# The ending of a fused attention and gated-MLP kernel: one bank for the last P V sum, two row tiles held in PSUM, stores from ScalarE, and a new written order

## The chip, the cores and the metric

The kernel runs on one core of a Trainium2 chip. The metric is the device time of one execution in microseconds. Before the change it was 691.36 us (median of 3 runs, 690.31 to 693.7).

## What is computed

With `x` of 2048 x 512 in bf16, 32 heads of 16 and a hidden width of 1792, the reference normalises each row and adds an attention block and a gated MLP block to the input:

```python
xn = layernorm(x)
q, k, v = split(xn @ wqkv)                      # 32 heads of 16
p = softmax(q @ k.T * 16 ** -0.5)               # per head, 2048 x 2048
attn = (p @ v) @ wo
h = relu(xn @ W_gate) * (xn @ W_up)
out = x + attn + h @ W_down
```

## The kernel before

Queries are taken in four chunks of 512 (`c4`), heads in four groups (`gg`) and in each the even and odd heads (`ee`): 32 blocks. In each block the keys go in 16 tiles of 128 (`kt`). TensorE works in "ops" of four matmuls of 64 rows by 32 columns, with one half of its rows (`half` 0 or 1, written by `matmul_loaded`, line 250); the two halves run side by side. Most key tiles are done as two *units*: two score ops write two PSUM banks (tiles `s`, two such pairs of banks), ScalarE takes the exponential of both banks in one instruction (line 1375) into a ring in SBUF, and two P V ops of each pair of units add to the block's sum. Other key tiles are *quads*: the exponential is made from integer arithmetic, by VectorE out of PSUM (line 1330), and then twice with a shift, on VectorE (line 1349) or GpSimd (line 1345); three times two P V ops use the results. There are 718 units.

The rest of TensorE's work, projections of q, k and v, gate and up (`gu`, `gg`) and the output rows (`ob`), is put between the scores. It shares four PSUM banks (pool `P_b`) with the quads' scores and the P V sums. Output row tiles of 128 queries sum the 14 parts of `h @ W_down` and four of `attn @ wo`, and the residual is added when VectorE takes them out.

The order of every engine's instructions is written out: `PLAN` is a packed list in which the operations that the code records are placed, with the buffer number of each tile. `Graph.run` reads it; `Graph.emit` adds the semaphores, and lets TensorE wait when an op of one half adds to a bank that the other half wrote last.

The ending (`normalise_last`, lines 1122 to 1181) belongs to the last block and the four row tiles of the last chunk:

- `LAST2 = 1`: the last block's P V sum is kept in two banks, one for each half (`tp`, `tp_hi`). ScalarE copies the one to SBUF (line 1148), VectorE adds the other (line 1150), each in two pieces of 256 queries.
- VectorE transposes in blocks of 32 (line 1153), takes reciprocals of the sums (1154), spreads them by a second transpose (1155) and multiplies (1157) into `qf`.
- All four row tiles were begun earlier (`out_rows`, `RN - 1` steps ahead of the end): the MLP parts and two head groups, taken out to `resid(i)` in fp32 together with `x` (line 1061). At the end two further groups (`oT`) and the normalised last one (`qf`) are projected by `stream_out` (line 1183) into the score banks `finA`, `finB`.
- Row 3 (`TAIL_ACT = (3,)`) gets its residual by an fp32 matmul with an identity matrix (line 1133) and is taken out by ScalarE (line 1171); rows 0 to 2 are added to their residual on VectorE (line 1174).
- SP issues the four stores (line 1179). Ahead of the last `LAST_STORES` entries of its queue it waits for all its other streams (line 498).

Of the kernel before, what the change touches and what calls it, by code (L numbers as in the profile page):

```python
# [13 lines left out]
ACTF = mybir.ActivationFunctionType  # L14
ALU = mybir.AluOpType

S = 2048
D = 512
H = 32
# [19 lines left out]
LAST_STORES = 4  # L39
# [15 lines left out]
LAST2 = 1  # L55
TAIL_ACT = (3,)
# [65 lines left out]
PLAN_OPS = 8251  # L122
PLAN = (
    "c-n1S1z;3c*PZibve|?P-r(+~K+zK1H53RgAq1zmLkq#JcySHx1oxuBixj8DwYa1-B)jwe``*m#&hq_5vOD|azANXP`<5z-?|)qU;npkhm-SBk%JG0+=1?9OFU$$t_)PpZ9&?`sx#E46{UQBP9-7;D"
    "=UY><D-W!Pig#D;eI!lD@z7?SVte7W#hl8mH{2Y<&EH({?qk_vJk!1JbU6Uxh2039E8-c%vSJ}9=1|2uRL+(k$TwoF?)3*vle5jk`|RXB47Z)yv>w(`bYn$sZK+tBadS6gynJfzO!nxW@#3W%C*Hxc"
    "ndc<Zc%8%A0<@vrlU5V2<p?fc$c16c1<%op4Qx@OC)|n$yk0f-l-r20y6IiHJv_N#`igVzO&o6d%sho*yJ47cl5RRc7|&g*VX%1=V+#)H9wQ*S&tK-YhNrk`mN3eg%&l{apQbZ~&E|n%_{j_vJ#(qL"
    "xrwyPo^@8V%qUxd;I?08&KMgT>sqNt&yBn^?6TZui>Y@5g?kFlc<;5*zK+~aJaj{*h+NNY#aa5(*g{w-=P8~-)6MvEFLIb$nihDA&-_ehT<qkr+8n1d`BZvZymYBzTW0KFd~TjdSf(&ru5s^CVXJcK"
    "RGMu*)0JdZ1cMn-;o>KqQhX#{x|w018>X>t=7zLNF6cIg%lU3$wtPS@nOn@43%E@ix#>g8|Gq~0;-IVnCOjz?7Uwm6&5ivm=ef<Gh!@f-Zfs{5F1%xyXyl3<z|GUjI3+9G&+s;6Qo?k%*ukwBM=-ZF"
    "wi0vQ=0@^k={C=~L}0%7*+JcljEap>JQ;75zaktfgX(6+AF;lhK4hk!6%%y0X9Rc40+Zzk6Aa8vbZ{Fncru?nDJMfNV5}iZg_&S1kL1ByGrEj}jAK^(4QowbTHE=Q1tc6v_lw%0K}im(e9#}$@j9d#"
    "w1``7W~7?P8pEZA>#Z0XhFd3>Kind}xM`)^f<422Yg5yFSjKwT!&aBx^y3~bv%#p1c;rX?KYu03UtvZ{ySZhK=@wz7=_=EcrhB+mMr7-kK$lp~JgB*pfvW%c3kq->Mwr$cCb%V6FuNKc&$!`13DZwr"  # L130
    "KoG_ln8CU7Rl+FD#z<}>V#W}zo7F9oO$Lb@Oy$98-AsF$!u2Gl;)N|w&Jd+=CSh1SW88vP4-c3&$gK^!qXW8CxjO8mDbb31M3{{%%}4O&tBXl1-Cvwv!@ZXVIJb!;?qvrb81igp{cRT^Uiwh%WNcg9"
    "qiuZFv#T|0F!!nti9lYY(CyMkx5-gUs+iDXI@wnIx)<>cZ_2eilq?s6$AhMLfK3b9>*Oo_YVHir@ja)~&EfFTY*xs=QhMe((7jY(LYqAvcI|Cty>3GtYfso5<Pk`UO|bfmvxJ0V-_S$JG6trYG$sll"
    "h2qgzoPVX6y+Jlt5WevHg0E8MD_XX3pGWg@?jxOTTE)_L7EgOnfm>{4(U3)wZtJH&U`xUnU}%)N#a+f8;<3(rgsLDqD~Q&{ZkU8?aFb*<YnBub@F6nYKofW{*VbHdPmvib7-?<DIsvN|hH?{7JhW?!"
    ";T~|em`6g1xt1Y2EtE6i%&a(WE@zzIKrZo?d|;f=l)Y|6F(sg+53YM%PV~jC_?m=fY;8<eEHPy;odt6S|H2rpc#zImSFv%wCI1bE<`z&|OUkj_FxsX2nI`KNLYs>lde#zj+)__wBA8Khd)gOce?!D6"
    "-WE&rN|txIQL@aCTZ$Juy@+byyyER3xYXfB=U_=LuBC9@t$9nq&29aOxA%}81$=5vHy{#Lhhvc|M4Bm3d^%LF*!y0Oru3Z0RQ$G+dnK`z^PU#hI+7VYGjw*KG=-1iZEk$jgGV5Fouhciac?mzwnR~M"
    "PwNU3`xR>qt6{NH5*FGk%2z<j?TxKzgSUg?RySqzGsY-xCM>t|*2f)YV+^k$rmnXT$j$(|oyiUM&_(DtcWE{U+3z|$ROZ9Ewo`E*8uvoF4Z!S|A<9={xDO0@KC!LttpM9eyo_Q2nn}1Y!9mAY*G9TW"
    "4#1OG#v)#KaZevBk>2b(J)B@#=W(h>F(f&doh41LNFL?pe&)*Hw)-d}XJn*3J9vf~lT49kp2#ki$=)P?FWm{L$$dK-#ix1o`PfFB);N1ZY>8~^uE{3Uz4^d>T6sGG+t;wfm0fb#<(iKbc7U-r$=vpo"
    "dm3@WCEUv?rg|40fL&I5FkOcY11zHER<k5A$3sz8S1a3i8?hRCiyPQ%u4qVgPy6fL$O1E1_-3)3hb0ZT<=)1@rXTSCl#}_^twXfo+@Yj+F~s^|Zsny<t0yoa-o$5%tY8N+DMj3t_HtXdZ1&SyTHiu%"
    "&yARQzr;=da_^;<mkxF7R?X;%JtPee(D}Mh_w*MQ{c+E&pA8H=O^=Zl9<^Za2W*PR7fS3&Y5=@(Il_IK4=azDM>AMGr`(;Jj*}6$dUaDc**Mo0An7=h>ukwkiyE_u4AUMvf!J=%cnV_{ohhdFGsKjU"
    ";)+Lf=$`cBp61V_eCw*vWLCMXMs}O`dL{{Zu3W9ev4U!a&$@r`5H`F-CC=xeFxwTQbq#8<w#8nyYe-8;dNhZX1G)*Ba)NGguSaAlU*FgJP?opN@=~rv!2c^CylCVBGhYc|-iTUv)0PypF`bV^+{T6}"  # L140
    "+SkNpmk!+9)Y$LrxSdXXNRs<>jMg@~?+rM&ci6V0amDvr79T@=klafQP`<L;D>FP_S$KOrPh)IAxWTDV{vUerwBPcT=dQtGeb`*4+nC<Q`d&gc?>!8($5&U<y0_uB)xEv;b!%tiX8J2y;^wyq_A5S*"
    "W$?sK_jZxo?t0yP2TNOWZo4n`Dlg+k)&3op&n3xM{LU4xLv{GveOTwyVRJUO-Q#@q6_ocH#rGCnw{A7K_5F>MBC^!2t1)g~eVG^8Ci$5cjn>Vs+um0i;A!=Q%yxmOSeI~&TNktj_>zi}&6Vf&O|fpA"
    "ty^kOZo94Coxx??HhVJKxYe}o#Ke`aX^5pbOqjPIUAI~m?g0zqytc0#yeaMZuFSZbfCtR%z-N73<i&6acHDDSZr$+dibaZ^mPhy82iaOT4+~ffWVR@V%2iCbGnmR~;e41{u{U=f3Q)kkU}q4x`Td^M"
    "xhB*Yt10;ZC8=*K!0j++YnZ@&uETu3KJ~O9%2)Vff9cbC_~ItFe+O#2jDz=EWZ&<8?f7P|GmfvAL9t!SnU`wb!&-1?C5LgdWsDPE{NF}Q@zE+i;A0e@r=o4&+xawDHstobjQyW6#+{12v-=9$^%OrJ"
    "p5WXLdR{cNU-)vLcz?~s_AA@3zht+k3IFQy+2#c$9en?L<bWgPU#O&&SrMqZs_JKpYg)h;RS!tU+fdD4eS&m&lL7u>ct*|b@2205>$$bR7@p>$XMQgFi_uRpAjJKarDyDBZq322;sJer4|##?456PG"
    "QqeXlzf|&ES)8RkaTWDhrIkR=N+&C^y|fDbq+dt^s<Q=USg5W|@4%Kv0VN!FfLsp8M@_uQ=FmR;1BChAep!D{Eth=cOmtpJNvw9H=4&8Rvijzmmk7mK*WQSBt4Hzse`&pb0ZyXcUK|?_Xbi(Av%#}~"
    "Pu=SvatqqVH^!$#_|NMb1ibY-z}fYAz<FFKjZ?2P`~-~prVRF^)!(IM<w^s?TCr7HyYGSiZC!y&R6Y7NtB7MYfOAQj^RtsioJe*$-9G?5TRK+g-IL1#2SS#+Sa(<K1z^`NwGK7-{zo8Q`=#EFT7g?1"
    "0%w~t2O0DyP(auEcPZ3=3L75@Ov%dbWq)#Z2e55k^r{xoK%EwA+Npk8b71AN4l6q?@IM3$DZp+Qxl&Y3-3eIrLfex7jMp-}OAH(ejM(#|7W7v4!$@F0-fn9&3MkeTY<=66H-NG0XY}%4azGmaOiU?t"
    "Ds`f^0_c?a$uNxD0J7%59~~FuoCY-0x+bj}j1uBisf*nML5D9h<=A$Xa~tq|&O3SU<;P~AXqkvn_-$2tQ~;ubSf5cLiLoeoF)u>UCeiUZBvCyJRPfi5aRjKg@?H>9em)FTnufHUk|+JF{tj$+rlCao"
    "_9jV1^5aC;P2EvoI`A6F9a0Le0$My;i(&V&UjjlM)gR@+ok0Eb6<`ngkN?F{lm;a99)l5+-6t#YAp<)AMSf$w=Tt^9@^Q!H!<Uo7_cG}9o&xPt{HI{Zm$mfji^}MXC`#$t!R5d##y|dY1}GmF?OHs4"  # L150
    "A<%sRdY>ugf2KklW!m?3Ci#`vN`}lvCp|!04@5v+-*!shoxo%CoSF)UY5_U!xqF-h9<=Pbd}E~g$3x`6Xss>cW&*p1Yn$Jp{lZ%L{>E`MZg`|J)xZxgvOjV8WqR#m>#HBB7RFr}_N1k!XK-r3Enu=X"
    "SNGRCP&f;^60onzF%)fe6UciK6<r;dINQ$!?mi0?Rg8MT@4fe;){<`5LCeQ1bF5~c5-K0Anm`k>1mntMRDT3y){kTC&d1r|JceJ!G5*V8l6(9m*0KT6rcjQ2(ry*Li*Kn43O+z4?PGD^C^9|S-~CPI"
    "O80=QY<MGFZ#UxXDzR36*WZO*4;Xp%Att_0Q*(W*gRdWFxliLBE?UR5<&+NRkop5I-)g;aLfF%+c)7HlwsZz?@fBvYa<j~sF@ZL?{3!EV>}cntH2YJZ?PMKU`m4zL3@w4?U5X<m3-Aw;t~zcOP=m{j"
    "8HF)jF!v|qe&j|jgtcAUQr{c^+(EV{$iQw^rNP&eg7T{wfgOPhyQRF_(0574MV)E`Eql)Dm(+|3kxuzJ^+!i5+V8dlB`&L+|2v1O=PA-ZKUw7JYP}0>Jx<fxBDt{`{#k3jx;3y<Pu7wG(P&pgY;<M6"
    "=bw(&Ox%?fbg(Z?D9`lo9T?hh4dGVwz-dcv=ezqKWdapGnr-2QihZQOHf#~;ayHV>i4dW1#$(%DtVMa?RQl&o93N<lt=QP=WVl;fH6LXEk-|8(jw)?48a};zl+_?)c>4~g%j4e={dixXX{9zu+_999"
    "b{S$=6<wp3TarqhFL#O%qjjS-(=PqD(eF#)WP;yP8|vvH<&Kx9kW4FovK-TB+i?!G&I&9RA-Y?Dzxp(e0AzE^me??f41bFiEDD5fflW3yXQT6_0Q<0N(y*nSRz6^}DTsey?N9Fz=%fg~>5M^4&F-d1"
    "trK;8t!N)YnWxo`La*Lej3rNv%X{ZcnG3rKn%X<DB>xy7QtLNIhu_ZNMAT_dWKttX<-^Iqb3~W=32g}A4o~Vn=luHCw=ayy6x|uPjmdg>c7}@Z6pmM!REnJ`<vhMeOjyzx<+pq!XpQW8;(9#L<Uj&O"
# [97 lines left out]
class Graph:  # L255
# [124 lines left out]
    def emit(self, nc, es):  # L380
# [93 lines left out]
        def play(e, eng):  # L474
# [953 lines left out]
```

## Time and profile before

| | |
|---|---|
| median of 3 runs | 691.36 us (690.31 to 693.7) |
| the profiled execution | 692.29 us |
| its span, first to last instruction | 690.4 us |
| TensorE, matmuls | busy 680.9 us, 22,248 records |
| ScalarE | busy 670.5 us |
| VectorE | busy 603.0 us |
| GpSimd | busy 499.3 us |
| exponentials, line 1375 | 718, first at 11.0, last at 679.4 us |

Matmuls are pipelined and their ends are modelled, so TensorE's busy share is not its share of peak. A row of the timeline gives start, length, engine, line, operation, the names of what is written and read, and in brackets the idle time before it with the engine that ended it. In a row of groups the number after the bar is busy time and mean length. The chain is followed back from the last instruction, each step to what released it.

### The profile page before, as it was taken

The page shows a single profiled execution, that of the slowest core. Times are in us where ns is not written, and L with a number is a line of the kernel's source. Part 1 is how long each engine was busy: PE and PEld are TensorE (multiplying, and loading weights), DVE is VectorE, ACT ScalarE, POOL GpSimd, SP SyncE. Part 2 cuts the span into 40 slices and gives each one's busy share as a digit, 9 for nine tenths or more (in the row PEclk, how much of TensorE's full clock was granted, in tenths as well). Part 3 has the DMA queues.
Part 4 walks back from the last instruction along what each step waited for, and adds up shares of the span by engine and source line. Part 5 has one row for each costly group of instructions (what it writes and reads, how often), then busy time and mean ns, then how long its engine had stood idle before and what let it go on. Part 6 is the DMA issues. An engine that isn't in the chain of part 4 may idle for free.

```text
span 690.4 us, 45217 instructions
## 1 busy us (share of the span) xinstructions
PE 680.9 (99%) x22248; PEld 357.3 (52%) x19848; DVE 603.0 (87%) x1017; ACT 670.5 (97%) x731; POOL 499.3 (72%) x507
## 2 busy tenths in 40 slices
PE   8999999999999999999999999999999999999997
PEld 4455555545545555555444565544554455555463
DVE  9958899999989788999999788989998887988876
ACT  6999999999999999999999999999999999999994
POOL 3223669777788778878677885988878778786791
PEclk9999999999999999999999999999999999999999
DMA  7330121021222021201200022030211013030111
GB/s 214 47 75 21 50 75 52 8 77 52 72 81 56 22 70 31 80 23 28 70 23 26 19 61 73 20 90 6 65 42 33 12 45 95 18 104 23 29 31 59
DMA packets 55941, 35.87 MB, mean 52 GB/s; under 512 B 19336, under 2 KB 51784, under 8 KB 55752
## 3 DMA queue, kind: packets, MB, share of 16 engines
q1 hardware_dynamic: 55752, 32.97, 17.4%
q8 instruction: 165, 2.70, 1.7%
q14 instruction: 24, 0.20, 0.1%
HBM read 26.35 MB, written 2.35 MB: 42 GB/s over the span
## 4 chain that ended last, share of the span: by engine, by line
PE 94%; DVE 4%; issue 1%; DMA 0%; POOL 0%; DVEq 0%
PE ps L250 94%; DVE qd L1330 1%; DVE stats L724 1%; DVE xn_sb L737 1%; DMA x_sb<-in_A_x_dram 0%; DVE hT L1017 0%; DVE qd L1349 0%; DVE xnT L778 0%; POOL rstd L719 0%; PE ps L1133 0%; DVE mv L725 0%; DVE xn_sb L1174 0%; DVE up_sb L1013 0%; DVE kT L866 0%; DVEq L514 0%
## 5 line engine op out<-in xcount | busy, mean ns | idle before, releaser
L1375 ACT ACTIVATE ring<-ps 128x1024 bf16<-128x1024 f32 x718 | 664.0, 1099 | 5.5 <-PE ps L250 4.1
L1345 POOL TENSOR_TENSOR qd<-qd,ints 128x512 int32<-128x512 int32 x446 | 450.0, 1039 | 157.3 <-DVE qd L1349 95.7
L250 PE MATMUL ps<-qT,kT 64*32 64x512 bf16 x8192 | 458.2, 374 | 1.0 <-DVE qd L1330 0.2
L1330 DVE TENSOR_SCALAR qd<-ps 128x512 int16<-128x512 f32 x612 | 397.8, 685 | 55.0 <-PE ps L250 50.5
L250 PE MATMUL ps<-qd,v_aug 64*32 64x512 bf16 x3672 | 267.2, 375 | 0.2 <-issue 0.2
L250 PE MATMUL ps<-ring,v_aug 64*32 64x512 bf16 x2872 | 237.7, 375 | 0.8 <-DVE kT L866 0.6
L1310 PEld LDWEIGHTS <-kT 64*32 64x32 bf16 x7676 | 156.7, 92 | 125.1 <-issue 33.0
L1282 PEld LDWEIGHTS <-v_aug 64*32 64x32 bf16 x4660 | 111.3, 91 | 70.7 <-issue 17.3
L250 PE MATMUL ps<-xnT,wgs 64*32 64x512 bf16 x1792 | 138.1, 374 | 0.3 <-issue 0.2
L250 PE MATMUL ps<-xnT,wus 64*32 64x512 bf16 x1792 | 137.8, 375 | 0.0
L808 PEld LDWEIGHTS <-wgs 64*32 64x32 bf16 x1792 | 43.3, 91 | 32.2 <-issue 8.0
L250 PE MATMUL ps<-Wd,hT 64*32 64x512 bf16 x768 | 57.7, 375 | 0.8 <-DVE qd L1330 0.7
L808 PEld LDWEIGHTS <-wus 64*32 64x32 bf16 x1792 | 43.6, 91 | 28.8 <-issue 6.2
L1349 DVE TENSOR_SCALAR qd<-qd 128x2048 int16<-128x2048 int16 x83 | 56.4, 690 | 1.9 <-PE ps L250 1.7
L808 PEld LDWEIGHTS <-hT 64*32 64x32 bf16 x1792 | 41.7, 92 | 30.1 <-issue 6.4
L250 PE MATMUL ps<-Wv,hT 64*32 64x512 bf16 x512 | 45.2, 375 | 0.0
L250 PE MATMUL ps<-Wk,hT 64*32 64x512 bf16 x512 | 43.5, 375 | 0.0
L1017 DVE SCALAR_TENSOR_TENSOR hT<-ps,up_sb 128x512 bf16<-128x512 f32 x56 | 38.4, 685 | 5.6 <-PE ps L250 5.1
L1013 DVE COPY up_sb<-ps 128x512 f32<-128x512 f32 x56 | 38.4, 685 | 3.3 <-PE ps L250 2.9
L250 PE MATMUL ps<-Wo_p,x_sb 64*32 64x512 bf16 x480 | 39.7, 375 | 0.5 <-issue 0.4
L250 PE MATMUL ps<-xnT,Wq 64*32 64x512 bf16 x480 | 36.0, 374 | 0.0
L250 PE MATMUL ps<-xnT,Wk 64*32 64x512 bf16 x480 | 34.6, 374 | 0.5 <-DVE xnT L778 0.3
(72 smaller groups left out, 266.3 us busy)
## 6 DMA issues: line engine op xcount, KB each, us to landing
rb<-rec_scr SPq DMA_DIRECT2D x31, 256.0 KB
wus<-in_B_W_up_dram SPq DMA_DIRECT2D x38, 128.0 KB, 3.1
wgs<-in_B_W_gate_dram SPq DMA_DIRECT2D x38, 128.0 KB, 3.1
xr_sb<-in_A_x_dram SPq DMA_DIRECT2D x16, 128.0 KB, 2.9
out_dram<-xn_sb SPq DMA_DIRECT2D x16, 128.0 KB, 2.2
qT<-qf SPq DMA_DIRECT2D x120, 16.0 KB, 2.8
x_sb<-in_A_x_dram SPq DMA_DIRECT2D x8, 128.0 KB, 2.4
x_sb<-oT SPq DMA_DIRECT2D x60, 16.0 KB, 2.7
```

Source lines behind the costliest of these rows:

```text
L250: return e.add_instruction(mybir.InstMatmult(name=e.bass.get_next_instruction_name(), engine=mybir.EngineType.PE, ins=[e.lower_ap(x), e.lo ...
L724: G.op("DVE", 580, lambda e, m=m: e.bn_stats(stats[:, m, :], xs(m)), reads=[t_xm[m]], writes=[t_st], prio=pr, order=last_xn if m == 4 else ())
L737: G.op("DVE", 320, lambda e, m=m, t=t_n: e.tensor_scalar(xn_sb[:, t.slot, :], xs(m), mv[:, m, 0:1], rstd[:, m:m + 1], op0=ALU.subtract, op ...
L808: e.ldweights(w()[rows, 32 * j:32 * j + 32], tile_position=(rows.start, 32 * j))
L1013: G.op("DVE", 603, lambda e: e.tensor_copy(up_sb[:, tup.slot, :], bank_of(tu)), reads=[tu], writes=[tup], prio=-590)
L1017: G.op("DVE", 603, lambda e: e.scalar_tensor_tensor(out=hT[:, th.slot, :], in0=bank_of(tg), scalar=0.0, in1=up_sb[:, tup.slot, :], op0=ALU ...
L1282: e.ldweights(vs(j), tile_position=(64 * half, 32 * j))
L1310: e.ldweights(ks(m), tile_position=(64 * half, 32 * m))
L1330: G.op("DVE", 601, lambda e, j=j, tx=tx: e.tensor_scalar(qd[:, tq.slot, 512 * j:512 * j + 512], ps[:, BANK[tx.slot], :], IBIAS[3], 0.0, op ...
L1345: G.op("POOL", POOL_NS / POOL_PIECES + 60, lambda e, x=x, n=n, c=slice(i * m, i * m + m): e.tensor_tensor(x().bitcast(I32)[:, c], raw().bi ...
L1349: G.op("DVE", 600, lambda e, n=n, x=x: e.tensor_scalar(x(), raw(), float(SHIFTS[n + 1]), None, op0=ALU.add), reads=[ti, tq], writes=[t], p ...
L1375: exp_ops[u] = G.op("ACT", 904, lambda e, tr=tr, k0=k0: e.activation(ring[:, tr.slot, :, :], ps[:, 4 * k0:4 * k0 + 2, :], ACTF.Exp, scale= ...
```

## The change

Four things change.

1. **One bank.** `LAST2 = 0`: the last block's sum goes to one bank, as the other blocks' do. The ScalarE copy and the VectorE addition are gone; the transposes and the products read the bank.
2. **Rows 1 and 3 stay in PSUM.** `TAIL_ACT = (1, 3)`. For these rows `out_rows` adds `x` by two ops with the bf16 identity, and doesn't take the tile out; its `flags` count on, so that the ops of `stream_out` for the last groups go on adding to the same bank. Their chains are recorded after those of rows 0 and 2, and their ops with `oT` need not wait for the last P V ops. The fp32 matmul is gone. Rows 0 and 2 use one pair of score banks.
3. **Stores.** VectorE adds and SP stores rows 0 and 2. ScalarE takes out rows 1 and 3 and issues their stores itself, on a semaphore `stored` for which SP waits at its end. `LAST_STORES` is 2.
4. **The written order.** `PLAN` is new for the whole kernel (8248 operations placed, 8251 before). Up to the 447th TensorE instruction the orders agree; behind it, all engines but ScalarE have another order. Counts by kind are the same but for the ending.

```diff
-LAST_STORES = 4
+LAST_STORES = 2
-LAST2 = 1
-TAIL_ACT = (3,)
+LAST2 = 0
+TAIL_ACT = (1, 3)
-PLAN_OPS = 8251
+PLAN_OPS = 8248
...
+        self.stored = es.enter_context(nc.semaphore("stored"))
...
+                eng.wait_ge(self.stored, 16 * len(TAIL_ACT))
...
         def out_rows(c4, i, gs, first, last, slots=None, pr=0.0, tile=None, sub=0):
+            held = c4 == NB - 1 and i in TAIL_ACT
...
+            if held:
+                pairs.append((lambda: ident[:], lambda: xr_sb[:, txr.slot, :]))
+                left = [2 * len(pairs) + 6]
+
+                def flags(n=left[0]):
+                    left[0] -= 1
+                    return left[0] == n - 1, left[0] == 0
+                mm_chain(t, pairs, reads + [txr, t_id], pr, slots=slots, flags=flags)
+                kept[i] = t, flags
+                return
...
-            for i in range(4):
+            for i in range(4) if c4 < NB - 1 else sorted(range(4), key=lambda i: i in TAIL_ACT):
...
         def normalise_last(tp, tp_hi):
-            tA, tB = Tile("finA", P_sc, [0]), Tile("finB", P_sc, [1])
-            rows = [(tA, 0), (tA, 1), (tB, 0), (tB, 1)]
+            free = Tile("finA", P_sc, [NU % 2])
+            rows = [(free, 0), (kept[1][0], 0), (free, 1), (kept[3][0], 0)]
...
-                    o = G.op("PE", 860, lambda e, i=i, t=t, sub=sub: e.matmul(bank_of(t, sub), identf[:], resid(i), start=False, stop=False),
...
-                G.op("ACT", 300, lambda e, c=c: e.activation(up_sb[:, tup.slot, c], at_bank(tp)[:, c], ACTF.Copy), reads=[tp],
-                G.op("DVE", 340, lambda e, c=c: e.tensor_tensor(o_sb[:, tos.slot, c], up_sb[:, tup.slot, c], at_bank(tp_hi)[:, c], ALU.add),
-                G.op("DVE", 340, lambda e, c=c: e.transpose(flip(c), o_sb[:, tos.slot, c]), reads=[to], ...
+                G.op("DVE", 340, lambda e, c=c: e.transpose(flip(c), bank(c)), reads=[tp], ...
-                G.op("DVE", 340, lambda e, c=c: e.tensor_tensor(oTl()[:, c], o_sb[:, tos.slot, c], up_sb[:, tup.slot, c], ALU.mult),
+                G.op("DVE", 340, lambda e, c=c: e.tensor_tensor(qf[:, tl.slot, c], spread(c), bank(c), ALU.mult),
...
+                    if i in TAIL_ACT:
+                        G.op("ACT", 566, lambda e, t=t, sub=sub, to_=to_: e.activation(xn_sb[:, to_.slot, :], bank_of(t, sub), ACTF.Copy),
+                             reads=[tf, t], writes=[to_], prio=-900 + i)
+                        G.op("ACT", 100, lambda e, store=store: store(e).then_inc(G.stored, 16), reads=[to_], ...
+                        continue
```

More of the change, by code (lines that the diff above doesn't have):

```diff
@@ L1023, in bass_parallel_sum__mha_block__glu_gated_reglu__prompt_kernel @@
         t_oT = {}
-        t_res = {}
+        t_res, kept = {}, {}
         glu_last = []
@@ L1136, in normalise_last @@
                 for n, (tg, wo) in enumerate(((t_oT[(3, 2)], lambda: Wo_p[:, 2, :]), (t_oT[(3, 3)], lambda: Wo_l[:, 0, :]))):
-                    for o in stream_out(t, sub, i, lambda tg=tg, i=i: oT_of(tg)[:, 128 * i:128 * i + 128], wo, [tg], n == 0, False, NU + 5 + i):
-                        o.order |= set(pv_ops[part(keys[-1])][-2:])
-            tl = Tile("oTl", P_qf)
-            oTl = lambda: qf[:, tl.slot, :]
-            at_bank = lambda t: ps[:, BANK[t.slot], :]
-            tot, tup = Tile("ot", P_o), Tile("up", P_up)
@@ L1144, in normalise_last @@
-            flip = lambda c: o_sb[:, tot.slot, c]
+                    for o in stream_out(t, sub, i, lambda tg=tg, i=i: oT_of(tg)[:, 128 * i:128 * i + 128], wo, [tg], n == 0 and i not in TAIL_ACT, False, NU + 5 + i, i not in TAIL_ACT):
+                        if i not in TAIL_ACT:
+                            o.order |= set(pv_ops[part(keys[-1])][-2:])
+            to, tup, tl = Tile("o", P_o), Tile("up", P_up), Tile("oTl", P_qf)
+            bank, flip, spread = lambda c: ps[:, BANK[tp.slot], c], lambda c: o_sb[:, to.slot, c], lambda c: up_sb[:, tup.slot, c]
@@ L1153, in normalise_last @@
-                G.op("DVE", 340, lambda e, c=c: e.transpose(flip(c), o_sb[:, tos.slot, c]), reads=[to], writes=[tt] if h else [tot, tt], joins=[tot] if h else [], prio=-949 + 10 * h)
+                tt, tr, ts, tn = (Tile() for _ in range(4))
+                G.op("DVE", 340, lambda e, c=c: e.transpose(flip(c), bank(c)), reads=[tp], writes=[tt] if h else [to, tt], joins=[to] if h else [], prio=-949 + 10 * h)
                 G.op("DVE", 190, lambda e, c=c, h=h: e.reciprocal(rlast[:, 8 * h:8 * h + 8], flip(c)[:, DH - 1:256:32]), reads=[tt], writes=[tr], prio=-948 + 10 * h)
-                G.op("DVE", 340, lambda e, c=c, h=h: e.transpose(up_sb[:, tup.slot, c], rlast[:, 8 * h:8 * h + 8].unsqueeze(2).to_broadcast([128, 8, 32])),
-                     reads=[tr, to], writes=[ts], prio=-947 + 10 * h)
@@ L1177, in normalise_last @@
-                    for k, w in enumerate(to_.w):
-                        d = slice(512 // len(to_.w) * k, 512 // len(to_.w) * (k + 1))
-                        dma(lambda e, m=m, to_=to_, d=d: e.dma_start(out2[128 * m:128 * (m + 1), d], xn_sb[:, to_.slot, d]), 128 // len(to_.w), reads=[], writes=[Tile()],
-                            prio=NU + 20, stream=("out", m % 8, k))
-                        G.ops[-1].deps[w] = True
-        def stream_out(t, sub, i, w, wo, reads, start, stop, prio):
+                    tf, to_, m = Tile("fin%d" % i), Tile("ost", P_xn, [i]), 12 + i
@@ L1184, in stream_out @@
+                    G.op("DVE", 603, lambda e, i=i, t=t, sub=sub, to_=to_: e.tensor_tensor(xn_sb[:, to_.slot, :], bank_of(t, sub), resid(i), ALU.add),
+                         reads=[tf, t_res[m]], writes=[to_], prio=-900 + i)
+                    t.r.append(G.ops[-1])
+                    dma(store, 128, reads=[to_], writes=[Tile()], prio=NU + 20, stream=("out", m % 8))
+        def stream_out(t, sub, i, w, wo, reads, start, stop, prio, late=True):
             made = []
             for half in range(2):
-                fn, load = chain_part(w, wo, lambda: bank_of(t, sub), half, lambda first=start and not half, last=stop and half: (first, bool(last)))
+                fn, load = chain_part(w, wo, lambda: bank_of(t, sub), half, kept[i][1] if i in kept else lambda first=start and not half, last=stop and half: (first, bool(last)))
@@ L1187, in stream_out @@
                 new = not t.w
                 o = G.op("PE", 216, fn, reads=reads + [t_wo, t_wol], writes=[t] if new else [], joins=[] if new else [t], prio=prio, mode="half", half=half,
-                         bank=(t, sub), after=NU if start else None, load=load, weights=reads)
+                         bank=(t, sub), after=NU if start and late else None, load=load, weights=reads)
                 if (t, sub) in fin_prev:
```

227 lines of the change are left out of this document (105 added, 122 removed).

## The prediction

> **What bounds the kernel now.** I read the page's first part, then the stretches of the span, the group of the exponentials and the chain that ended last, and last the timeline of the ending.
>
> ```profile
> span 690.4 us, 45217 instructions
> PE 680.9 (99%) x22248; PEld 357.3 (52%) x19848; DVE 603.0 (87%) x1017; ACT 670.5 (97%) x731; POOL 499.3 (72%) x507
> ```
> ```profile
> 11.00:100.00 89.00, 87.39 (x2791) 46.41 (x2638) 73.61 (x135) 87.45 (x95) 37.43 (x46) 1.00 0.29 66
> 400.00:500.00 100.00, 99.88 (x3411) 52.95 (x3004) 90.51 (x148) 99.88 (x110) 81.28 (x81) 1.00 0.19 53
> 600.00:679.40 79.40, 79.19 (x2720) 43.98 (x2403) 65.71 (x107) 78.20 (x86) 60.52 (x60) 1.00 0.17 49
> ```
> ```profile
> L1375 ACT ACTIVATE ring<-ps x718: 1018/1086/1282, 11.0 to 679.4; 128x1024 bf16<-128x1024 f32 x180
> ```
> ```profile
> by line: PE ps L250 94.2%; DVE qd L1330 1.4%; DVE stats L724 0.8%; DVE xn_sb L737 0.6%; issue 0.5%; DMA x_sb<-in_A_x_dram 0.3%; DVE hT L1017 0.2%; DVE xnT L778 0.2%; DVE qd L1349 0.2%; POOL rstd L719 0.2%; PE ps L1133 0.2%; DVE mv L725 0.1%
> ```
>
> In a row of a stretch stand start, end and length, then the busy time of PE, PEld, DVE, ACT and POOL with counts, the granted clock, and the DMA's share and GB/s. ACT does one thing from 11.0 to 679.4 us: 718 exponentials, 717 steps in 668.4 us, 0.932 us a step. In the best stretch it does 110 in 99.88 us, 0.908 us each. At that pace the train would last 717 x 0.908 = 651.0 us, so 17.4 us of the train are steps in which ACT had to wait for scores. TensorE delivers these: the chain is 94.2% TensorE, and 0.5% of it is "issue" (3.45 us in which it waited for nothing that the profile shows) and 1.4% is the quad conversion on DVE (9.7 us). So there are three parts: 11 us of start, the train of 668 us, paced by ACT and stretched by TensorE, and an ending of 10 us. The change rewrites the ending, and it re-orders the train.
>
> ```profile
> 679.36 1.10 ACT L1375 ACTIVATE ring<-ps 128x1024 bf16<-128x1024 f32 x1
> 681.09 0.66 ACT L1148 ACTIVATE up_sb<-ps 128x256 f32<-128x256 f32 x2 [0.63 <-PE ps L250]
> 681.63 0.75 DVE L1150 TENSOR_TENSOR o_sb<-up_sb,ps 128x256 f32<-128x256 f32 x2 [0.99 <-PE ps L250]
> 682.30 0.44 DVE L1153 STREAM_TRANSPOSE o_sb<-o_sb 128x256 f32<-128x256 f32 x1
> 683.60 1.12 PE L1133 MATMUL ps<-xnT,identf 128*128 128x512 f32 x2
> 683.65 0.43 DVE L1157 TENSOR_TENSOR qf<-o_sb,up_sb 128x256 bf16<-128x256 f32 x1
> 684.47 0.42 DVE L1157 TENSOR_TENSOR qf<-o_sb,up_sb 128x256 bf16<-128x256 f32 x1
> 684.69 0.38 PE L250 MATMUL ps<-Wo_l,qf 64*32 64x512 bf16 x4
> 685.82 1.89 DVE L1174 TENSOR_TENSOR xn_sb<-ps,xnT 128x512 bf16<-128x512 f32 x3 [0.93 <-PE ps L250]
> 686.61 1.93 SPq L1179 DMA_DIRECT2D out_dram<-xn_sb  x4
> 687.01 0.60 ACT L1171 ACTIVATE xn_sb<-ps 128x512 bf16<-128x512 f32 x1 [5.26 <-PE ps L250]
> ```
>
> The last exponential ends at E = 679.36 + 1.10 = 680.46. From there: ACT copies one partial sum, DVE adds the other, and the first transpose starts at 682.30 (E+1.84). The first normalised half is ready at 683.65 + 0.43 = 684.08, but its first projection starts only at 684.69 (E+4.23): TensorE is in the f32 residual matmul until 684.72. The row results leave from 685.82; SP sends four stores one behind the other until 688.54, and the span ends at 690.4, E+9.94.
>
> **The change part by part.** An "op" below is four matmuls on one 64-row half of the array; 22,248 / 4 = 5562 of them. The rows show the rate:
>
> ```profile
> 678.99 0.38 PE L250 MATMUL ps<-qd,v_aug 64*32 64x512 bf16 x4
> 679.10 0.38 PE L250 MATMUL ps<-Wv,hT 64*32 64x512 bf16 x4
> 679.21 0.38 PE L250 MATMUL ps<-qd,v_aug 64*32 64x512 bf16 x4
> 679.31 0.38 PE L250 MATMUL ps<-Wo_p,x_sb 64*32 64x512 bf16 x4
> 679.43 0.38 PE L250 MATMUL ps<-qd,v_aug 64*32 64x512 bf16 x4
> 679.53 0.38 PE L250 MATMUL ps<-Wo_p,x_sb 64*32 64x512 bf16 x4
> 679.64 0.38 PE L250 MATMUL ps<-qd,v_aug 64*32 64x512 bf16 x4
> ```
>
> Six steps in 0.65 us: an op each 0.108 us when the halves alternate, and 0.216 us from one op to the next of the same half (679.10, 679.31, 679.53).
>
> *The sums without the ACT copy and the DVE add.* The two L1148 copies and two L1150 adds go; both transposes read the one bank. A transpose from PSUM isn't in the trace. The nearest rows are these, and all three cost the same whether PSUM or SBUF is read, so I take the same 0.42 us (ends: nothing, and 0.1 us more each):
>
> ```profile
> L1157 DVE TENSOR_TENSOR qf<-o_sb,up_sb 128x256 bf16<-128x256 f32 x2 | 0.9, 426 | 0.0
> L1153 DVE STREAM_TRANSPOSE o_sb<-o_sb 128x256 f32<-128x256 f32 x2 | 0.8, 418 | 0.0
> L1150 DVE TENSOR_TENSOR o_sb<-up_sb,ps 128x256 f32<-128x256 f32 x2 | 0.8, 418 | 1.0 <-PE ps L250 1.0
> ```
>
> But in the one bank the halves have to take turns. In the new written order the last exponential's P V op on the upper half is followed by six ops of the lower half up to the end of the sum, two of row work, three of a quad tile and the last P V op: with the first of them started at about E+0.1, the sixth starts at E+0.1+5 x 0.216 = E+1.18, and 0.38 later, with a release of about 0.1, the transpose starts at E+1.65. If TensorE is a few ops behind by then, it is E+1.95. I take E+1.8: the copy and the add are nearly given back. The first product is then ready at E+1.8+1.78 = E+3.6 (before E+3.62).
>
> *Rows 1 and 3 in PSUM.* The f32 matmul (1.12 us) goes from the ending; four ops with the identity come in (0.43 us), and two L1061 evictions of 0.68 us leave DVE, where they lie beside the train and cost nothing (DVE is idle 13%); if they mattered, they give back 1.4 us at most. In exchange, row work that stood ahead of the last P V op now fills TensorE's gap under the DVE steps: 19 ops between the last P V op and the first projection of the normalised half, 13 of them on the upper half. 13 x 0.216 = 2.8 us from E+1.2 is E+4.0, and a wait between halves of one bank adds about 0.3. So TensorE, not DVE, is late next: first projection at E+4.15 (before E+4.23). Ends: E+3.7, set by the product, to E+4.6.
>
> *Stores.*
>
> ```profile
> L1179 SPq DMA_DIRECT2D out_dram<-xn_sb x4: 332/338/430, 686.6 to 688.1; - x4
> DMA to landing us min/median/max: 1.7/1.7/1.8
> ```
> ```profile
> L1057 SPq DMA_DIRECT2D out_dram<-xn_sb x12: 357/613/1978, 282.6 to 675.8; - x12
> ```
>
> Row 3 left ACT at 687.01+0.60 = 687.61, but its store was issued at 688.1 behind three others: 0.5 us lost on SP. Now DVE takes rows 0 and 2 and SP their stores, ACT takes rows 1 and 3 and issues theirs itself. After the first projection the last row's op still stands behind six ops of the lower half and a change of half, about 2.05 us; 0.42 to ACT, 0.60 for the copy: store issue 3.1 us after the first projection, against 3.4 before. That is -0.3. What an issue costs on ACT isn't in the trace: between nothing and SP's longest, 1.98 us; I take SP's 0.34, as before. Ending: -0.1 - 0.3 = **-0.4 us**; with the ends, -1.2 to +1.6.
>
> *LAST_STORES and the semaphore.* SP's list of waits stands ahead of the last two stores instead of four; behind it only these two are queued. Before, the first store started 0.1 us after its row was ready, so it costs nothing; were it late, only row 0 would be.
>
> *The order of the train.* The work is the same, and so is each engine's count; 9 fewer ops stand ahead of the last score (5517 against 5526). What changes is where TensorE stalls. The "issue" part of the chain is 3.45 us, 0.55 of it in the ending, so at most 2.9 us are there to be had from better places for stalls without a cause in the profile; I take half, **-1.5 us**. The 9 ops are worth 9 x 0.108 = 1.0 us if TensorE sets the last step; from 600 us on ACT is busy 78.20 of 79.40 us, so I take none.
>
> Sum: -1.5 - 0.4 = -1.9. The profiled execution took 692.29 us (span 690.4 and 1.9 around it), 0.9 above the median of 691.36; so 690.4 for it, and **689.5 us** for the median.
>
> **What speaks against it.** Counted in the written orders, runs of ops on one half have lengths 1, 2, 3, 4, 5 in numbers 2596, 1102, 200, 41, 1 before, and 2064, 994, 356, 98, 10 after. Runs of three and more nearly double, 242 to 464. A step has 5562 / 718 = 7.75 ops, 0.84 us against ACT's 0.908: one lost slot of 0.108 us in a step already makes it late.
>
> **The rivals.**
> - *The order pays.* All 2.9 us of issue go, and a third of the 9.7 us behind the quad conversion: 2.9 + 3.2 + 0.4 = 6.5, **684.9 us**. For it: 17.4 us of the train are late steps. Against it: the same engines keep the same counts, and only 3 us have no cause in data.
> - *Long runs starve the other half.* If an op can pass only one waiting op, a run of n loses n-2 slots: 156 + 2 x 57 + 3 x 9 = 297 more, of 0.108 us, 32 us; if it can pass two, 57 + 2 x 9 = 75 slots, 8 us. I take 20. TensorE needs 5562 x 0.108 = 601 us of the train's 668, 67 idle, of which 17.4 show as late steps, a quarter. A quarter of 20 is +5; with the ending **696.0 us**. It decides from the one lost slot per step above. Against it: in the seven rows above three row ops of one half (679.10, 679.31, 679.53) stand in a row in the written order, ahead of two of the P V ops between them, and they cost nothing.
> - *The array keeps strict order.* Then each run of n >= 2 takes n-1 times 0.216 us: 632 us before, 663 after, +31: **722 us**. The same rows speak against it: 679.21 starts ahead of 679.31, which stands first in the order. The Trainium skill, "TensorE: Matmul & The Clock Gate", section "The mechanism", states just that rule: matmuls start and end in program order, with no reordering. Here the rows disagree.
> - *The ending doesn't shrink:* ACT's store issue costs 1.98 us, +1.6, and the train gains 1.5: **691.3 us**.
>
> **How the numbers follow.** Forecast 0.44, order pays 0.27, long runs 0.22, strict order 0.02, ending 0.05. A measurement can tell about 0.5%, 3.5 us: 687.9 to 694.8. Forecast and ending lie inside, so same 0.49, faster 0.27, slower 0.24. The forecast's own range is 688 to 692. To leave out 2 in 10, the range runs from just below the paying order to 2 us above the long runs: 684 to 698.
>
> **What would show it.** First transpose at E+1.65 to E+1.95; first projection at E+4.15 with no f32 matmul before it; last store issued at E+7.2 by ACT. The train's length says which order case holds: 667 us for the forecast, 662 if the order pays, 673 and more exponentials ended by "PE ps" if long runs starve a half. It is wrong if the start differs from 11.0 us, or if ACT's store lands later than 1.8 us.

## The result and the profile after

The changed kernel takes **699.96 us** (median; 699.79 to 700.32), the kernel before 691.2 in the same comparison: a ratio of 1.0122, 95% interval 1.0095 to 1.0148. It is slower by about 8.5 us, above the prediction's range of 684 to 698. The profiled execution took 700.32 us, with a span of 698.4.

The page's first lines, the stretches of the span, the exponentials' line and the chain by line, all of the kernel after:

```profile
span 698.4 us, 45185 instructions
PE 686.6 (98%) x22259; PEld 364.2 (52%) x19806; DVE 602.9 (86%) x1012; ACT 674.6 (97%) x730; POOL 499.8 (72%) x507
```
```profile
11.00:100.00 89.00, 87.73 (x2812) 48.46 (x2650) 73.82 (x135) 88.03 (x96) 37.72 (x46) 1.00 0.29 66
400.00:500.00 100.00, 98.78 (x3320) 54.27 (x2936) 87.72 (x143) 98.31 (x107) 80.27 (x80) 1.00 0.19 53
600.00:687.50 87.50, 87.27 (x2944) 46.41 (x2588) 73.67 (x119) 86.01 (x94) 65.42 (x64) 1.00 0.16 43
```
```profile
L1366 ACT ACTIVATE ring<-ps x718: 1017/1042/1277, 11.0 to 687.5; 128x1024 bf16<-128x1024 f32 x180
```
```profile
by line: PE ps L251 88.4%; ACT ring L1366 5.9%; DVE qd L1321 1.8%; issue 0.5%; DVE up_sb L1017 0.4%; DVE stats L727 0.3%; DMA x_sb<-in_A_x_dram 0.3%; POOL qd L1336 0.3%; PE ps L765 0.2%; ACT qT L952 0.2%; ACT xn_sb L1165 0.2%; POOL rstd L72
```

The start is the same (11.0 us) and the clock is full. The train of exponentials runs from 11.0 to 687.5: its unrounded length (last start less first) is 676.45 us, where it was 668.36. So **+8.1 us are in the train**, all that the span grew by (690.4 to 698.4, rounded). In the first stretch nothing is lost (96 exponentials instead of 95); behind it the loss grows bit by bit: the train is 2.7 us behind at the 300th exponential, 5.1 at the 500th, 8.1 at the 650th, and the stretch from 400 to 500 holds 107 exponentials instead of 110. "Issue" is 0.5% of the chain, as before. The waits of the two kernels that pass between TensorE, VectorE and ScalarE (total us, times, longest), first before, then after:

```profile
DVE qd L1330 <- PE ps L250: 50.5, 114, 1.2
ACT ring L1375 <- PE ps L250: 4.1, 11, 0.8
PE ps L250 <- DVE qd L1330: 0.9, 2, 0.7
```
```profile
DVE qd L1321 <- PE ps L251: 51.6, 117, 1.3
ACT ring L1366 <- PE ps L251: 6.4, 19, 1.0
PE ps L251 <- DVE qd L1321: 2.6, 9, 0.8
```

ScalarE waits for scores 19 times instead of 11, and TensorE for VectorE 9 times instead of 2. These waits are only the idle time between rows, and the rows of neighbouring exponentials overlap; the steps from one exponential's start to the next show all of the loss. Half of the steps take 0.905 us or less in both kernels; those over 0.95 us are 93 before and 126 after. The work is the same and so is the undisturbed step, so the question is why the same operations, in another order, come later.

The ending, from the timeline after (start, duration, engine; rows left out):

```profile
686.56 2.00 ACT L1366 ACTIVATE ring<-ps 128x1024 bf16<-128x1024 f32 x2
690.55 0.45 DVE L1152 STREAM_TRANSPOSE o_sb<-ps 128x256 f32<-128x256 f32 x1 [2.42 <-PE ps L251]
691.91 0.42 DVE L1156 TENSOR_TENSOR qf<-up_sb,ps 128x256 bf16<-128x256 f32 x1
692.54 0.38 PE L251 MATMUL ps<-Wo_l,qf 64*32 64x512 bf16 x4
```
```profile
693.46 0.69 DVE L1169 TENSOR_TENSOR xn_sb<-ps,xnT 128x512 bf16<-128x512 f32 x1 [0.32 <-PE ps L251]
694.25 1.89 SPq L1163 DMA_DIRECT2D out_dram<-xn_sb  x2
694.59 0.38 ACTq L1163 DMA_DIRECT2D out_dram<-xn_sb  x1
695.70 0.43 ACTq L1163 DMA_DIRECT2D out_dram<-xn_sb  x1
```
```profile
DMA to landing us min/median/max: 2.1/2.7/3.0
```

The last exponential ends at E = 686.56 + 2.00 = 688.56, and the span at 698.4, E+9.84; before it was E+9.94. The ending got at most 0.1 us shorter.

### The profile page after: what moved, and what is told of

It reads as the page before. It is cut to its first block, busy times and chain, and to the rows that moved or that the text cites. A ratio compares the mean times of both kernels' runs of the same rounds, so it can differ in the third digit from the quotient of the medians.

```text
span 698.4 us, 45185 instructions
## 1 busy us (share of the span) xinstructions
PE 686.6 (98%) x22259; PEld 364.2 (52%) x19806; DVE 602.9 (86%) x1012; ACT 674.6 (97%) x730; POOL 499.8 (72%) x507
## 4 chain that ended last, share of the span: by engine, by line
PE 89%; ACT 6%; DVE 3%; POOL 0%; issue 0%; DMA 0%; ACTq 0%; POOLq 0%
PE ps L251 88%; ACT ring L1366 6%; DVE qd L1321 2%; DVE up_sb L1017 0%; DVE stats L727 0%; DMA x_sb<-in_A_x_dram 0%; POOL qd L1336 0%; PE ps L765 0%; ACT qT L952 0%; ACT xn_sb L1165 0%; POOL rstd L722 0%; PE ps L927 0%; PE ps L1381 0%; DVE xn_sb L740 0%; DVE hT L1021 0%
## 5 line engine op out<-in xcount | busy, mean ns | idle before, releaser
L251 PE MATMUL ps<-qT,kT 64*32 64x512 bf16 x8192 | 462.9, 374 | 3.6 <-DVE qd L1321 1.0
```

The lines of the kernel that those rows point to most:

```text
L251: return e.add_instruction(mybir.InstMatmult(name=e.bass.get_next_instruction_name(), engine=mybir.EngineType.PE, ins=[e.lower_ap(x), e.lo ...
```

## The experiments

Five theories stood against each other. **R**: long runs of one 64-row half starve the other half (the prediction's third case). **W**: scores of quads stand too close behind the conversion that frees their bank. **F**: the order hangs on the places at which TensorE would have to stop for the fetch of its instructions. **S**: the order has too little lead for short stops. **Q**, formed after the first two groups of runs (a1, a2, s1; a4, b2, a5, hyb): operations of the two halves *start* out of the written order, but *report their end* in it. Some expectations give an estimate from a replay: the five written queues played through with durations from the traces (0.216 us an operation, 0.9035 a step of ACT, 0.60 a step of a conversion).

Only TensorE's written order (PLAN) is edited unless a diff shows code; in hyb the queues of VectorE, GpSimd and SP change too. Each diff below is one place of the written order, cut out as an example; a number tells the unit or quad. "Row sum" is an operation of the output rows' sums, "pair score" one for an exponential, "quad score" one for a conversion on VectorE. Ratios are to the kernel before. The length of a train comes from the one profiled execution of a kernel, and executions of one kernel differ (b2: 686.11 to 690.01 us), so a difference of 1 to 3 us between two trains has the right order of size and no more; the ratio with its interval decides.

### Long runs broken (a1)

```diff
-half 1  P V 252
 half 1  P V 252
 half 0  row sum
 half 1  P V 252
+half 1  P V 252
```


> The changed kernel with its runs of one half of TensorE's rows broken: 224 operations of the other half brought forward by one to three places into runs of three and more, no score of a quad moved (runs of three and more: 465 before the edit, 213 after). Theory R (long runs starve the other half, the prediction's third case): in the replay of the written order with the traces' durations, where an operation may start only once the second before it has started, the train gets 5 us shorter; 695 us, train 671. Theory W (the order is late for VectorE, runs don't matter): train within 1 us of 676.5, 699 to 700. Theory S (the order has too little lead to absorb the short stalls of TensorE): 1.5 to 2.5 us shorter, 697.5 to 698.5.

697.52 us, ratio 1.0098 (1.0078 to 1.0117); the train 674.94, -1.5 us against the changed kernel. The ratio's interval overlaps with that of the changed kernel (1.0095 to 1.0148), so the gain itself isn't clear of noise. R asked for -5, 695 us or a ratio of 1.006, which lies below the interval. -1.5 is the size that S gave.

### Waiting quad scores moved later (a2)

```diff
 half 0  P V 255
+half 0  pair score 261
 half 1  quad score 266
-half 0  pair score 261
```


> The changed kernel with the 105 quad scores that its trace shows waiting for VectorE moved later by as many operations as would have fitted into their wait (214 places in all). Theory W (these scores stand too close behind the conversion that frees their bank, and hold up both halves while they wait): TensorE fills the waits, 4 to 6 us shorter, 694 to 696 us. Theory R: no change, 699 to 700. Theory S (the scores are late, not early: VectorE is waiting for them too, and later scores delay the conversions behind): 5 to 7 us longer, 705 to 707.

703.63 us, ratio 1.0183 (1.0161 to 1.0204); the train 681.75, +5.3. W is wrong, in sign: the scores for which VectorE waits are late already.

### Half a fetch further on (s1)

```diff
-            for _ in range(10):
+            for n in range(134):
+                e.ldweights(Wo_l[0:64, 0, 0:32], tile_position=(0, 32 * (n % 4)))
+            for _ in range(4):
                 ins = e.matmul(ps[:, BANK[0], :], Wo_l[:, 0, 0:128], zeros, start=True, stop=True)
```


> The changed kernel with 128 weight loads put ahead of its first matmuls (6 of 10 warming matmuls taken out), so that every later TensorE instruction stands half a fetch of 256 instructions further on; order unchanged. Theory F (the order is fitted to the places where the instruction fetch stops TensorE, and what it gains hangs on them): the train changes by 3 us or more, most likely longer, 703 or more. Theories R, W and S: train within 1.5 us of 676.5, the time moves only by what the loads delay the first exponential.

The instruction queue moved 165 packets in the kernel after:

```profile
q8 instruction: 165, 2.70, 1.7%
```

TensorE has 22,259 matmuls and 19,954 weight loads there, so that a packet holds about 256 instructions. The result is 701.37 us, ratio 1.0147 (1.0126 to 1.0168); the first exponential at 10.97, the train 678.42, +2.0. That is between the two forecasts, and the interval overlaps with that of the changed kernel: F's 703 or more isn't there, and that the places cost anything isn't shown. One shift doesn't settle it.

### Single moves in a replay with stops (a4, b2), and the control without (a5)

```diff
 half 1  quad score 266
+half 1  row sum
 half 0  pair score 261
 half 1  pair score 261
-half 1  row sum
```


> The changed kernel with the same instructions and queues of the other engines, and TensorE's operations in another order: single operations moved by up to eight places where that shortened the train in a replay of the order with the traces' durations that stops the instruction stream for 0.15 us every 256 instructions, averaged over 16 positions of that stop. Theory S (the changed order has too little lead to absorb short stops of the instruction stream, wherever they fall): the replay gives 13 us less for the train than the changed kernel, of which I expect 8 to 13; 687 to 692 us. Theory F (places are all): the order is fitted to no place, so no gain over the kernel before and at most 2 us over the changed kernel, 698 to 700. Theory R also forecasts a gain here, 10 us, since this order serves the halves evenly.

685.97 us, ratio 0.9946 (0.9927 to 0.9964); the train 661.93, -14.5 against the changed kernel. The same done to the kernel before:

```diff
 half 0  P V 255
+half 0  P V 253
 half 1  quad score 266
-half 0  P V 253
+half 1  row sum
 half 0  pair score 261
 half 1  pair score 261
-half 1  row sum
```


> The kernel before with TensorE's operations moved in the same manner as in a4 (stops of 0.15 us, 16 positions). Theory S: the replay gives 8 us less than for the kernel before; 683 to 688 us. Theories F and W: no gain, 690 to 693.

688.15 us, ratio 0.9979 (0.9963 to 0.9995); the train 664.91, -3.5: a gain, but less than half of what S forecast (8 us). The control:

```diff
+half 1  row sum
 half 1  row sum
 half 0  row sum
-half 1  row sum
 half 0  row sum
```


> The control to a4: the changed kernel's order moved by the same kind of steps, but by a replay without any stop of the instruction stream. Without stops the replay gives 2 us less than the changed kernel. Theory S: with stops of 0.15 us it gives 4.4 us more; 703 to 706 us. Theory R (an operation may start only once the second before it has started): 19 us more, 715 to 720. If stops don't matter: 697 to 699.

716.47 us, ratio 1.0388 (1.0365 to 1.0411). The exponentials' line and their wait in a5:

```profile
L1361 ACT ACTIVATE ring<-ps x718: 1018/1032/1153, 11.1 to 703.2; 128x1024 bf16<-128x1024 f32 x180
ACT ring L1361 <- PE ps L246: 15.1, 51, 0.9
```

The train is 692.19, +15.7. Moves that cost nothing in a replay in which an operation reports as soon as it is done cost 16 us on the chip, four times what S gives. R, with 19, is near, though a1 had gone against it. Something that acts like R, but isn't R, was missing.

### What the traces show of starts and reports

The example that shows it best is one score of a quad in the kernel after. The written order, with the half of each operation and the start that the trace gives it:

```
written   half   operation                start
4386      0      row sum   ps<-Wd,hT      552.476
4387      0      row sum   ps<-Wd,hT      552.691
4388      0      row sum   ps<-Wd,hT      552.907
4389      1      quad score ps<-qT,kT     552.515
```

The timeline of the kernel after at this place (the weight loads and one P V row left out):

```profile
552.24 0.40 PE L251 MATMUL ps<-qT,kT 64*32 64x512 bf16 x8
552.48 0.38 PE L251 MATMUL ps<-Wd,hT 64*32 64x512 bf16 x4
552.51 0.38 PE L251 MATMUL ps<-qT,kT 64*32 64x512 bf16 x4
552.69 0.38 PE L251 MATMUL ps<-Wd,hT 64*32 64x512 bf16 x4
552.91 0.42 PE L251 MATMUL ps<-Wd,hT 64*32 64x512 bf16 x8
553.37 0.69 DVE L1321 TENSOR_SCALAR qd<-ps 128x512 int16<-128x512 f32 x1 [0.83 <-PE ps L251]
```

The score starts at 552.51, ahead of two row sums that stand before it: its half was free, so the long run starved nothing. But the conversion that waits for it starts only at 553.37, 0.85 us after the score and 0.46 after 552.91, the start of the last *older* operation. VectorE stood idle for 0.83 us. All conversions that started on their score's report, in the traces of the two kernels and of three experiments (two of them below), sorted by whether an older operation started over 0.05 us after the score; medians in us:

| kernel | no older one later: n, from the score | an older one later: n, from the score | from the last older start |
|---|---|---|---|
| before | 202, 0.427 | 39, 0.642 | 0.475 |
| after | 181, 0.426 | 65, 0.702 | 0.477 |
| a5 | 126, 0.426 | 130, 0.725 | 0.482 |
| q1 | 148, 0.426 | 90, 0.652 | 0.476 |
| a7 | 220, 0.427 | 13, 0.591 | 0.477 |

Counted from the score, the second group scatters (0.56 to 0.93 between the tenth and the ninetieth percentile in the kernel after); counted from the last older start it is 0.46 to 0.50. And starts are not held up: where two or three older operations hadn't started yet (177 and 24 cases after, pair scores not counted), the operation started in the median at the moment at which its half was free, and on average 0.02 us later. So a run of one half doesn't delay the other half's work. It delays the news of it: Q.

The traces also hold the time of each semaphore increment, and they show this without the conversions. TensorE's operations report on four semaphores, among them one for each half. In the 14 traces of this case (3217 to 3239 reports in each) every report comes in the written order, across the halves too, without one exception. In the kernel after, a report comes 0.402 us (median) from the operation's start when no older one starts over 0.05 us later, and otherwise 0.445 us from the last older start. The score above started at 552.515 and was reported at 553.343. Summed over all quad scores, the time by which a report comes more than 0.402 us after the start is 23.4 us before, 38.7 after and 13.0 in a7 below. For the exponentials that start late on the report of their scores, about 6.5 us of the lateness before, 12.3 after and 4.0 in a7 is such a delay of the report: about 5.8 of the train's +8.1 us come by this way.

### Long runs that delay a report, and long runs that don't (q1, q2)

```diff
 half 1  row sum
+half 0  row sum
+half 0  row sum
 half 0  P V 252
 half 1  row sum
-half 0  row sum
 half 1  row sum
-half 0  row sum
 half 0  pair score 262
```


> The kernel before with TensorE's operations between the first and the 690th exponential moved by single places until 552 runs of one half are three or longer (242 in the kernel before), and so that many an operation that starts ahead of older ones is one for which VectorE or ScalarE waits. Theory Q (operations of the two halves start out of the written order, but report their end in it, so that an operation behind a long run starts on time and is reported late): the replay with ends in order gives 9 us more than for the kernel before, 11.9 with stops of 0.1 us; 698 to 703 us. Theory R (an operation may start only once the second before it has started): no change without stops, 4 us with them; 690 to 695. Ends not in order and no reach: 0.3 us, with stops of 0.15 us 5.8; 690 to 697.

703.76 us, ratio 1.0168 (1.0137 to 1.0199). The counterpart:

```diff
-half 1  quad score 266
+half 1  row sum
 half 0  P V 253
 half 0  pair score 261
+half 1  quad score 266
 half 1  pair score 261
-half 1  row sum
```


> The counterpart of q1: the kernel before moved in the same manner to as many long runs (590 of three and more, and longer ones: 26 of five against 6), but so that those for whom an engine waits are not behind older ones. Theory Q: no change without stops, 4.8 us more with stops of 0.1 us; 690 to 695 us, and clearly under q1. Theory R: 9 us more, 13.6 with stops; 699 to 704, and clearly over q1. If long runs as such cost (the prediction's third case), both lose alike, 8 us or more.

695.01 us, ratio 1.005 (1.0031 to 1.007). The exponentials in q1, then in q2:

```profile
L1372 ACT ACTIVATE ring<-ps x718: 1017/1030/1159, 12.0 to 691.4; 128x1024 bf16<-128x1024 f32 x180
ACT ring L1372 <- PE ps L247: 5.6, 15, 0.9
```
```profile
L1372 ACT ACTIVATE ring<-ps x718: 1018/1047/1192, 11.3 to 682.4; 128x1024 bf16<-128x1024 f32 x180
ACT ring L1372 <- PE ps L247: 4.1, 11, 1.0
```

The trains are 679.47 and 671.10: +11.1 and +2.7 against the kernel before. With as many long runs (590 of three and more against 552), and more of the longest, q2 loses a quarter of what q1 loses by the trains, and 0.5% against 1.7% by the times (in q1 the first exponential also comes 1.0 us later). R wanted the opposite, and the prediction's third case wanted both alike. Q gave 9 to 11.9 and 0 to 4.8.

### The order rewritten as the chip starts it (a7, b7)

The most direct test leaves the starts as they are and changes only whose report waits for whom:

```diff
-half 0  row sum
 half 0  row sum
 half 1  quad score 266
+half 0  row sum
 half 1  P V 253
```


> The changed kernel with its order rewritten as its own trace shows TensorE starting it: each of 725 operations that started over 0.05 us ahead of an older one is written ahead of it (878 places in all, 1.2 each; nothing else is changed). Theory Q (operations start ahead of older ones but report their end behind them): the starts stay, the reports come earlier; the replay gives 13.4 us less for the train, 16 with stops of 0.1 us; I expect 8 to 13 us less than the changed kernel, 687 to 692. If starts are all that matters (ends reported at once): within 1 us of the changed kernel without stops, at most 5 less with stops of 0.15 us, 695 to 700. Theory F (the places of the instruction fetch): the same, 698 to 700.

686.93 us, ratio 0.9928 (0.9904 to 0.9952): **13 us less than the changed kernel, and faster than the kernel before.** The page's line, the exponentials and the waits of a7:

```profile
PE 675.8 (99%) x22262; PEld 354.3 (52%) x19806; DVE 600.6 (88%) x1012; ACT 666.9 (97%) x730; POOL 499.0 (73%) x507
```
```profile
L1361 ACT ACTIVATE ring<-ps x718: 1018/1113/1315, 11.5 to 673.3; 128x1024 bf16<-128x1024 f32 x180
```
```profile
DVE qd L1316 <- PE ps L246: 45.0, 106, 1.1
ACT ring L1361 <- PE ps L246: 1.6, 4, 0.8
PE ps L246 <- DVE qd L1316: 1.1, 3, 0.7
```

The train is 661.75, -14.7. The same score as above, now written ahead of two of the row sums, in a7's timeline (cut):

```profile
540.52 0.38 PE L246 MATMUL ps<-Wd,hT 64*32 64x512 bf16 x4
540.53 0.38 PE L246 MATMUL ps<-qT,kT 64*32 64x512 bf16 x4
540.73 0.38 PE L246 MATMUL ps<-Wd,hT 64*32 64x512 bf16 x4
540.95 0.39 PE L246 MATMUL ps<-Wd,hT 64*32 64x512 bf16 x8
540.98 0.69 DVE L1316 TENSOR_SCALAR qd<-ps 128x512 int16<-128x512 f32 x1 [0.31 <-PE ps L246]
```

The score starts 0.01 us after the first row sum, as it started 0.04 after it in the kernel after. Its conversion follows 0.45 us behind it, not 0.85. The same done to the kernel before:

```diff
-half 0  P V 255
+half 1  row sum
+half 0  P V 253
 half 1  quad score 266
-half 0  P V 253
```


> The same done to the kernel before: 412 operations that its trace shows starting over 0.05 us ahead of an older one are written ahead of it (446 places). Theory Q: 2.9 us less for the train without stops, 4 with them; 686 to 689. If starts are all that matters: no change, 690 to 692.

690.03 us, ratio 0.9972 (0.9954 to 0.999), the train 665.81, -2.6: a small gain, slower than the forecast of 686 to 689.

### A further search with reports in order (a6), and the old train with the new ending (hyb)

This diff is against a4, from which a6 was made:

```diff
+half 0  row sum
+half 1  P V 253
 half 0  row sum
 half 0  row sum
 half 1  row sum
-half 1  P V 253
-half 0  row sum
```


> The changed kernel with an order made from a4's by further single moves, this time by a replay in which operations report their ends in the written order, without a stop and with stops of 0.22 us at 16 positions (runs of three and more: 133, in the changed kernel 465). Theory Q (ends are reported in order): the replay gives 14.4 us less for the train than the changed kernel without stops, and 2 us less than a4 with stops of 0.1 us; 683 to 685.5 us, faster than both kernels. If ends in order were not the cause, the order would be no better than a4's: 686 or more.

687.23 us, ratio 0.9939 (0.9918 to 0.996), the train 662.10: no better than a4. The 2 us that the replay gave for stops were not there. For hyb the written order is that of the kernel before up to the 641st exponential's scores (the diff is against the kernel before):

```diff
+half 1  wus
 half 1  wus
 half 0  P V 636
+half 0  pair score 641
+half 1  pair score 641
 half 0  wgs
 half 1  wus
-half 0  pair score 641
-half 1  pair score 641
-half 1  wus
```


> The changed program with the train's order of the kernel before up to the 670th exponential, and from there a transition to the changed ending (bank, kept row tiles and stores of ScalarE as in the change). If the loss is all in the order and the ending is worth its 0.1 to 0.4 us: 690.5 to 692. If the kept banks or the new ending cost the train something: 694 or more, with the loss after the 640th exponential.

692.95 us, ratio 1.0056 (1.0034 to 1.0078), above the forecast of 690.5 to 692. The train is 667.91, 0.5 less than in the kernel before: with the old order the loss is gone. But the time from the last exponential's end is 11.2 us, 1.3 more than in the kernel after, since the transition leaves row work behind the train. So hyb shows where the loss is, and doesn't price the new ending; a4 and b2, each with its own ending, do so better: both take 9.8 us behind the last exponential.

### All trains in one table

Change of the train's length in us, measured, and in three replays without stops: reports at once, reports at once with a start only after the second before has started (R), and reports in the written order (Q).

| kernel | against | measured | at once | R | Q |
|---|---|---|---|---|---|
| after | before | +8.1 | -0.1 | +7.2 | +10.1 |
| b2 | before | -3.5 | -0.2 | -1.2 | -3.4 |
| b7 | before | -2.6 | +0.5 | -0.5 | -2.9 |
| q1 | before | +11.1 | +0.3 | 0.0 | +9.0 |
| q2 | before | +2.7 | +0.4 | +9.0 | 0.0 |
| hyb | before | -0.5 | +0.2 | +2.4 | +1.9 |
| a1 | after | -1.5 | 0.0 | -5.1 | -3.3 |
| a2 | after | +5.3 | +7.6 | +7.1 | +4.0 |
| a4 | after | -14.5 | -0.4 | -8.7 | -13.7 |
| a5 | after | +15.7 | 0.0 | +19.2 | +14.5 |
| a6 | after | -14.4 | -0.4 | -8.7 | -14.4 |
| a7 | after | -14.7 | +0.2 | -8.1 | -13.4 |

Q is within 2.7 us in every row. Counted with reports at once the changed order is as good as the old one: by the replay, what it lost isn't work, nor stalls of its own, but late reports, 10 us in the replay for 8.1 measured.

## Why the prediction was wrong

- **What bounds the kernel:** right. The train is paced by ACT and stretched by TensorE, and all of the difference lies in it.
- **The sums:** the transposes from PSUM took 0.45 and 0.40 us (forecast 0.42). The first started at 690.55, E+1.99, just behind the forecast E+1.65 to E+1.95. The sum left out the change of half in the bank ahead of the last four P V operations: the one on the upper half started at 689.03, the next on the lower half, which waits for its report, at 689.48.
- **Rows 1 and 3 in PSUM:** right. The first projection of the normalised half started at 692.54, E+3.98 (forecast E+4.15, before E+4.23), and no f32 matmul stands ahead of it. The 0.3 us put in for a wait between halves came from no row; the 0.45 us of the change of half above, less a step of 0.11, bear it out.
- **Stores:** the last was issued by ACT at 695.70, E+7.14 (forecast E+7.2), and the issue took 0.43 us (0.34 taken). But from there to the end of the span it is 2.7 us, before 690.4 - 688.1 = 2.3, and these stores landed after 2.1 to 3.0 us where 1.8 was put in. That ate 0.4: the ending is worth -0.1, not -0.4.
- **LAST_STORES:** right. SP's first store went out at 694.25, 0.1 us after its row (693.46 + 0.69).
- **The order of the train, -1.5 us: this is the step that failed; it is +8.1.** It took "what changes is where TensorE stalls" for the whole effect, and the 2.9 us of "issue" for all that could change; "issue" is still 0.5%. The written order also decides when each operation's end is reported, and that had no term: it was put at nothing. After, 725 operations start over 0.05 us ahead of an older one and are reported behind it, before, 412 (those that a7 and b7 write ahead of it); writing the 725 ahead takes 14.7 us off the train.
- **The rival "long runs starve the other half":** its time, 696.0, was nearest and its +5 had the right sign, and it named the right count (242 to 464 runs); that it came near was luck. Its mechanism fell: starts aren't held up, a1 with half of the long runs broken gains 1.5 where 5 was asked for, and q2 with 590 of them loses 2.7. Its seven rows, in which overtaken operations "cost nothing", were read rightly for starts and say nothing of reports.
- **The rival "strict order":** it was weighed as one piece and thrown out by one row. The Trainium skill, "TensorE: Matmul & The Clock Gate", section "The mechanism", holds that matmuls start and end in program order. For starts on different row halves this case's traces disagree (552.51 ahead of 552.69). For ends, as the semaphores and the waiting engines see them, they agree: no report out of order in 14 traces, and a conversion 0.477 us from the last older start. Half of that rule is what the changed order ran into.
- **The count of operations:** 5562 takes in 119 matmuls of the whole array and of columns, which aren't operations on one half; 5532 are. It changes the sums by 0.5% and no conclusion.
- **The chances:** 0.24 for slower was too little; the case that came true stood in none of the rivals.

What stays open: whether the end itself or only its report is held back (the trace models the ends of matmuls, so it can't tell); whether the places of the instruction fetch are worth anything (s1: +2.0 us in one profiled execution, not clear of noise); and the train's last 14 us over ACT's own pace (661.75 against 717 x 0.9035 = 647.8), which no replay without stops has.

## What to carry to other kernels

On TensorE, write operations in the order in which they will start: an operation that slips past an older one on the other half starts early but is known to be done only behind it. Take the starts from a trace, write the order so, and measure again; here that turned a loss of 1.2% into a gain of 0.7%, and gave the kernel before 0.3%. When an order is searched in a model, ask what the model believes of the *report* as well as of the start: the control a5 was free in such a model, and cost 16 us.

## What was not expected of the hardware

- Starts of matmuls on the two 64-row halves pass up to three older ones with next to no delay (0.02 us on average); reports pass none, in 14 traces: 0.426 us from a score to its conversion when nothing older is behind, 0.477 from the last older start otherwise. A semaphore for each half doesn't change that.
- A store issued by ACT took 0.38 to 0.43 us of it, and the ending's stores landed after 2.1 to 3.0 us, not 1.8.
